# A convolution kernel's parameter ladder and first table put under an order searched offline

## The chip, the cores and the metric

The program runs on one core of one Trainium2 chip. The metric is device time in microseconds (us). Four runs of the kernel before spread from 529.19 to 531.01, so differences of a few microseconds in 530 need several runs.

Five engines matter here. PE multiplies matrices (PEld is its loading of weights), DVE works on vectors, ACT works elementwise and evacuates PE's results, POOL and SP do little (before, POOL is busy 2% of the span and the page lists no busy time for SP). In these traces an engine takes the instructions of its queue in their order, and the queues meet at semaphores: before, DVE waits 2.08 us at its first statistics, up to 9.29 us, and the square of sh behind them, whose input was ready at 7.87, starts at 11.08. So the order in a queue decides what waits for what.

## The reference

The program is a stack of four layers on a sequence of 2048 rows and 512 channels: a long convolution, a local attention, and both again. Each layer works on the normalized rows and adds its result to them.

```
x = x + conv(layernorm(x))       # this change: layernorm and the start of this layer
x = x + attention(layernorm(x))
x = x + conv(layernorm(x))
x = x + attention(layernorm(x))

# the convolution's kernel, for each channel d and lag l, over 128 modes n:
K[d, l] = Re( sum over n of  C[d,n] * dt[d]*B[d,n] * exp(dt[d]*(A_re + i*A_im)[d,n] * l) )
# and the convolution itself by Fourier transforms of length 2L
```

## The kernel before

The first 64 us prepare two things. The **ladder** squares the complex base exp(dt A) ten times (`lad`, 128 x 512 numbers each for the real and imaginary part) and casts each power into multipliers (`MU`, `MUA`, `MUB`, `MP`, `MH`). The **tables** hold powers by lag for 64 channels at a time, eight tables in all; a table is a seed, four doubling levels (two products and a sum each), a fifth "high" level, and three products `y`. PE then contracts a table with 256 small matmuls (`psk`) to 64 rows of the convolution's kernel. A table lies in one of two buffers:

```python
class Tables:
    def __init__(self, nc, tc, es, M, cb):
        self.tt = es.enter_context(tc.tile_pool(name="t_t", bufs=2))   # two buffers for eight tables
    ...
    def seed(self, hc):                    # the first DVE operation on table hc
        self.nc.vector.tensor_copy(self.T[hc][:, 1, :, :, 0, :]..., self.cb[:, hc]...)
```

The work from the tables to the end of the convolution is written as a plan: operations with an engine, a duration, and the buffers they take and drop. An offline search picked an order and, for some, one of two engines; the kernel only carries the numbers of the operations in that order.

```python
def tables(hc):
    o = pl.op("G", 0.4, lambda: T.ones(hc), take=[("T", hc)])          # takes one of the two buffers
    o = [o, pl.op("V", 0.15, lambda: T.seed(hc), o)]
    for lev in range(4):
        ab = pl.op("V", ..., lambda lev=lev: T.level(hc, lev), o)
        ...                                                            # levels 2 to 4: sum on DVE, or on PE and ACT
def contract(hc):
    for half in range(2):
        a = pl.op("P", 2.9, mm, ...)                                    # 128 matmuls
        e = moved(pl, nc, ("psk", hc, half), 0.5, 0.61, evac, a, ...,
                  drop=[("psk", hc, half)] + ([("T", hc)] if half else []))   # the buffer is free here
```

Ladder and norms were outside the plan, in hand-written order; tables 0 and 1 were both in it, level by level in turn.

Of the kernel before, what the change touches and what calls it, by code (L numbers as in the profile page):

```python
# [192 lines left out]
def load_params(nc, pp, prm):  # L193
# [16 lines left out]
    "33 58 34 59 35 60 36 61 37 62 38 63 39 64 40 66 43 1 44 55 4 49 56 50 5 67 57 2 7 8 10 68 83 32 11 12 69 22 18 "  # L210
    "84 86 80 19 74 20 87 81 90 89 78 21 155 15 79 76 16 27 25 91 77 92 26 93 82 94 115 95 96 97 118 116 100 101 30 "
    "119 189 121 123 112 31 156 126 124 190 132 106 127 129 154 130 191 108 133 113 109 145 139 110 146 135 111 147 "
    "192 136 150 114 151 137 148 193 214 138 194 195 196 152 215 199 157 153 163 217 158 200 164 211 159 218 205 161 "
    "160 259 220 142 324 162 260 143 209 212 175 171 210 166 180 172 207 167 173 261 208 168 262 263 174 178 213 169 "
    "186 183 179 185 292 264 284 184 187 221 293 188 265 237 298 285 295 299 301 266 287 296 323 269 302 308 270 223 "
    "288 318 358 281 239 225 290 359 229 313 227 360 231 241 325 275 243 311 233 235 361 321 245 312 303 277 322 362 "
    "279 278 282 316 280 247 317 363 326 251 283 332 249 333 253 327 364 383 254 365 368 256 384 369 328 257 330 386 "
    "380 329 331 374 334 350 387 306 381 351 432 389 497 340 307 352 341 353 342 433 375 345 357 343 337 434 346 355 "
    "382 465 338 347 466 468 354 435 457 414 469 348 436 390 356 471 458 437 460 472 438 439 442 392 461 531 463 498 "
    "416 532 443 396 394 533 474 454 418 475 496 534 406 420 477 481 492 478 535 408 486 493 398 536 479 410 448 412 "  # L220
    "494 480 400 495 537 484 449 404 402 489 485 456 425 490 499 426 538 503 455 500 422 504 505 423 501 502 541 559 "
    "506 517 429 562 507 560 542 556 553 513 547 563 520 514 565 608 523 521 510 554 524 529 515 511 525 548 516 527 "
    "526 555 528 609 611 610 530 613 566 612 615 614 629 616 558 622 567 557 617 569 630 635 574 570 572 632 636 582 "
    "575 583 577 431 633 620 580 590 578 585 621 430 625 586 627 588 638 626 661 628 591 648 639 662 593 428 649 641 "
    "594 669 651 596 642 670 598 652 654 599 601 655 605 644 604 602 664 645 606 657 607 665 647 667 672 677 658 675 "
    "685 660 679 673 686 681 688 683 692 689 699 696 700 693 697 702 694 703",
    "39 20 40 1 21 22 41 2 58 3 23 59 42 4 30 10 60 11 61 6 7 16 66 28 13 17 64 35 26 49 14 24 194 68 32 43 101 62 "
    "195 45 47 126 72 102 79 127 54 76 80 104 51 77 85 105 75 82 86 107 83 228 110 108 229 112 113 244 88 115 248 245 "
    "89 119 246 249 230 120 247 94 232 122 252 231 233 250 91 96 253 236 92 251 97 141 234 256 237 142 235 98 258 254 "
    "259 257 100 255 116 240 242 123 117 238 243 125 241 239 169 260 223 170 264 262 224 272 263 265 138 274 284 273 "  # L230
    "139 157 285 275 278 158 129 132 286 130 268 279 133 135 287 266 269 136 151 288 267 270 152 160 289 154 276 161 "
    "271 290 156 277 291 163 280 296 144 164 332 172 282 145 283 334 176 147 333 319 338 177 148 335 320 149 166 340 "
    "339 167 188 321 344 341 189 191 322 336 345 192 185 323 201 337 346 186 197 324 173 342 198 347 174 325 297 343 "
    "179 348 326 298 180 365 350 182 371 351 366 183 367 202 352 200 372 353 203 368 331 220 354 379 217 221 211 355 "
    "375 218 380 212 208 356 369 357 376 205 209 303 370 206 358 214 226 311 304 215 359 227 312 309 364 310 301 299 "
    "302 305 300 307 306 385 308 391 316 313 389 318 386 373 315 392 377 390 395 378 374 381 393 396 383 397 394 384 "
    "399 398 429 387 400 430 388 421 401 431 407 404 403 432 409 408 406 433 422 411 434 410 413 412 499 437 415 414 "
    "500 438 417 416 439 497 419 418 440 498 420 441 442 503 423 456 446 501 426 425 444 504 443 502 428 457 448 445 "
    "505 447 450 507 449 452 508 451 454 525 506 461 509 465 453 510 526 455 511 463 462 512 475 458 466 464 469 476 "
    "473 470 513 467 460 474 471 521 519 481 479 517 468 480 522 485 482 472 515 486 483 523 477 489 491 487 484 524 "  # L240
    "527 493 557 528 529 553 530 558 531 573 494 545 554 532 575 533 488 572 586 534 546 587 574 535 492 561 576 588 "
    "490 549 577 536 495 563 578 540 537 607 589 542 590 580 609 550 598 543 562 599 582 604 591 600 564 605 608 565 "
    "618 606 610 619 611 612 620 621 613 566 622 614 617 623 567 624 570 628 568 625",
    "5 9 14 6 4 15 11 7 3 1 12 8 2 0 13 10 17 21 25 105 22 19 26 29 33 30 109 34 111 106 45 113 117 39 114 121 119 37 "
    "123 38 193 42 197 195 48 124 199 201 49 205 133 203 206 81 51 59 82 214 84 70 60 130 281 71 52 136 127 85 282 53 "
    "73 137 208 86 56 57 285 74 88 211 169 90 62 286 158 217 170 139 75 159 147 63 79 140 220 77 172 148 141 221 64 "
    "173 143 146 174 66 69 289 223 178 101 176 293 290 103 92 150 294 95 98 93 224 96 242 151 99 225 161 243 302 152 "
    "227 245 229 296 253 156 162 154 231 299 254 246 163 232 256 305 247 165 234 167 330 249 251 183 257 331 308 235 "
    "184 333 258 309 319 260 334 262 341 311 320 186 342 312 180 187 189 181 236 190 313 322 240 238 335 315 323 317 "
    "276 339 344 324 337 277 264 326 279 268 328 265 347 269 267 272 350 348 271 273 361 355 362 352 275 356 358 353 "  # L250
    "359",
    "1 20 2 3 58 21 4 22 59 39 8 6 11 9 40 13 23 60 41 24 16 26 14 30 32 61 42 28 17 197 47 49 45 35 79 62 198 64 43 "
    "126 68 80 51 66 76 127 54 101 77 104 102 75 85 105 72 82 86 107 83 228 88 108 229 90 91 230 110 93 232 231 94 "
    "112 233 244 113 96 245 236 97 114 119 234 237 248 120 235 98 246 122 252 249 99 247 250 144 242 251 253 238 243 "
    "116 146 254 239 123 118 256 255 166 125 258 257 167 169 240 259 171 241 160 260 182 161 264 262 183 266 263 265 "
    "157 272 284 267 158 129 285 273 278 130 163 151 286 164 274 172 279 152 148 287 270 275 149 132 288 271 268 133 "
    "138 289 154 276 139 269 147 155 290 277 291 135 280 185 296 136 332 173 186 282 338 174 333 283 194 346 339 319 "
    "195 176 340 347 177 179 320 344 341 180 191 200 321 342 345 192 205 336 343 206 188 334 337 189 211 201 297 335 "
    "212 214 348 322 323 298 215 305 324 350 223 303 351 306 224 299 352 325 304 353 326 300 354 331 202 355 309 217 "
    "203 307 310 218 141 356 311 357 308 142 301 208 358 365 209 302 226 359 312 369 366 313 220 364 316 370 315 375 "  # L260
    "221 318 385 376 391 386 227 387 392 393 388 389 394 377 390 399 378 395 400 397 396 407 398 379 404 401 367 406 "
    "380 408 373 403 368 371 374 419 372 381 415 520 383 417 416 384 521 420 429 413 511 430 499 411 414 431 512 418 "
    "432 500 505 433 421 434 412 506 409 435 422 436 410 441 528 448 423 442 501 426 425 450 454 443 502 449 529 428 "
    "455 446 451 444 516 513 456 447 452 445 461 457 467 453 517 462 458 468 469 524 473 463 460 475 474 525 470 464 "
    "476 465 560 471 530 479 466 472 481 480 485 477 482 483 486 489 548 493 484 491 549 487 492 550 539 531 540 488 "
    "532 543 535 544 494 536 490 554 495 547 555 561 556 566 562 567 568 572",
]


def flat(xs):  # L270
    return [z for x in xs for z in (flat(x) if isinstance(x, (list, tuple, set)) else [x])]


class Plan:


# [42 lines left out]
class Multipliers:  # L319
# [8 lines left out]
    def slots(self, k):  # L328
# [7 lines left out]
        if k % 6 == 0:  # L336
            return [self.one[:, :, 1 - k // 6].unsqueeze(3), self.base[1][:, 0, :, 1 - k // 6]]
        return [self.base[0][:, k % 6 - 1, :, 1 - k // 6], self.base[1][:, k % 6, :, 1 - k // 6]]


def ladder(nc, pp, pst, identf, raw, M, cb, fill):

# [72 lines left out]
    for i in range(11):  # L415
# [7 lines left out]
        if i == 0:  # L423
            coefs()
# [1167 lines left out]
```

## Time and profile before

| Before | us |
|---|---|
| time, median of 4 runs beside the changed kernel | 530.39 (529.19 to 531.01) |
| span of the profiled run | 528.9 |
| table 0 complete on DVE | 63.9 |
| first PE transposes of the attention layer | 226.1 |

The prediction below shows the busy times and the timelines of DVE and ACT. Three more views are needed. First the busy time by stretch (length, then busy PE, PEld, DVE, ACT, POOL with counts, then granted clock, DMA share, GB/s):

```profile
226.00:530.00 304.00, 268.64 (x1880) 142.71 (x1893) 263.50 (x451) 166.65 (x264) 4.78 (x40) 0.97 0.33 74
```

This is the stretch from the attention layer on, which the change should leave alone. Second, the waits of DVE, with the total, the number and the longest:

```profile
DVE prod L1241 <- ACT kT L1195: 15.0, 2, 7.6
...
DVE ln_st_b L150 <- ACT X L856: 3.3, 3, 1.9
```

Third, PE's timeline (start, length, operation, idle before and what ended it):

```profile
63.67 1.99 PE L711 MATMUL ps_s<-X,sb_F 128*128 128x128 bf16 x16 [6.31 <-ACT Z L716]
65.59 0.24 PE L558 MATMUL psk<-Ttab 128*32 128x64 bf16 x4
...
69.11 0.22 PE L558 MATMUL psk<-Ttab 128*32 128x64 bf16 x4 [0.74 <-issue]
```

The contraction of table 0 starts at 65.59, and DVE has table 1 to work on meanwhile. Inside the contraction PE stands still once, for 0.74 us, with nothing visible to wait for ("issue").

### The profile page before, as it was taken

To read this page: it belongs to the slowest core of one execution; us is meant where nothing else is said; L and a number is where in the kernel's file an instruction comes from. 1 tells how busy PE (TensorE), PEld (TensorE's weight loads), DVE (VectorE), ACT (ScalarE), POOL (GpSimd) and SP (SyncE) were. 2 spreads that over 40 slices of the span, in tenths; PEclk is the share of its full clock that TensorE was granted. 3 is DMA by queue.
4 is the path that set the end of the run, shared out by engine and by line. 5 is a ranking of instruction groups with operands and counts; after the bars stand their busy time and mean duration, and the time that the engine had idled before them with its cause. 6 is when DMAs were issued, how large, how long until landed. Compare 5 with 4: busy or idle time off the path is not lost.

```text
span 528.9 us, 11855 instructions
## 1 busy us (share of the span) xinstructions
PE 404.1 (76%) x4929; PEld 238.6 (45%) x4943; DVE 475.5 (90%) x803; ACT 339.2 (64%) x505; POOL 12.9 (2%) x62
## 2 busy tenths in 40 slices
PE   0201367799878779689999788969995999996896
PEld 0100235466655547443456234555673333652352
DVE  4999999999999998749899998889989497999995
ACT  3999965887857668662766137989995336651230
POOL 0000000000000004000000000000000000000000
PEclk9999997979989999979999999999996999999999
DMA  8300083249135343460011522779501400223242
GB/s 264 153 1 0 0 141 90 61 114 163 43 114 110 62 142 106 139 120 31 0 61 50 91 49 40 197 204 159 81 2 35 85 30 32 71 48 61 40 130 90
DMA packets 88922, 45.08 MB, mean 85 GB/s; under 512 B 74923, under 2 KB 81068, under 8 KB 88612
## 3 DMA queue, kind: packets, MB, share of 16 engines
q1 hardware_dynamic: 87284, 43.93, 34.8%
q8 instruction: 38, 0.62, 0.5%
q10 hardware_dynamic: 1584, 0.39, 0.4%
q14 instruction: 16, 0.13, 0.1%
HBM read 15.77 MB, written 8.13 MB: 45 GB/s over the span
## 4 chain that ended last, share of the span: by engine, by line
PE 34%; DVE 33%; ACT 10%; issue 9%; DMA 3%; SPq 0%; POOL 0%; DVEq 0%; ACTq 0%
PE ps_qk L1190 11%; DVE prod L1353 7%; PE ps_v L1210 4%; PE Lp L1251 3%; DVE Y2tab L545 3%; DVE Ttab L545 3%; DVE ln_st_b L150 2%; DVE Ttab L488 2%; DVE Ttab L481 2%; DMA Kt<-kt_scratch 2%; DVE Ttab L480 2%; PE ps_o L1426 2%; DVE prod L1241 2%; ACT X L598 1%; PE po L1374 1%
## 5 line engine op out<-in xcount | busy, mean ns | idle before, releaser
L1241 DVE TENSOR_TENSOR prod<-qT,kT 128x2048 bf16<-128x2048 bf16 (+1 forms) x80 | 77.1, 1005 | 15.7 <-ACT kT L1195 15.0
L1353 DVE TENSOR_TENSOR prod<-VX,L 128x2048 bf16<-128x2048 bf16 (+2 forms) x96 | 77.4, 861 | 1.7 <-PE po L1374 0.9
L1190 PE MATMUL ps_qk<-xnT,wqk 128*128 128x512 bf16 x256 | 63.7, 388 | 0.1
L1369 PE MATMUL po<-prod,sb_ident 128*128 128x512 bf16 x216 | 54.5, 378 | 8.1 <-DVE prod L1353 4.9
L1369 PEld LDWEIGHTS <-sb_ident 128*128 128x128 bf16 x224 | 21.4, 97 | 35.6 <-issue 11.7
L1190 PEld LDWEIGHTS <-wqk 128*128 128x128 bf16 x256 | 22.8, 100 | 32.1 <-issue 11.6
L1210 PE MATMUL ps_v<-wv,xnT 128*128 128x256 bf16 x256 | 34.6, 282 | 0.8 <-ACT xnT L1168 0.6
L1389 ACT CAST ot<-po 128x1024 bf16<-128x1024 f32 x14 | 13.6, 1014 | 29.7 <-PE po L1369 29.7
L520 PE MATMUL ps_sum<-Ttab,sb_ident 128*128 128x512 bf16 x18 | 8.3, 459 | 31.0 <-DVE Ttab L480 27.7
L1251 PE MATMUL Lp<-prod,sb_bones 128*32 128x512 bf16 x256 | 28.6, 388 | 4.3 <-DVE prod L1241 4.2
L1215 ACT CAST VX<-ps_v 128x512 bf16<-128x512 f32 x32 | 18.8, 587 | 17.2 <-PE ps_v L1210 17.2
L716 ACT CAST Z<-ps_s 128x1024 bf16<-128x1024 f32 (+1 forms) x32 | 29.4, 995 | 0.5 <-PE ps_s L711 0.4
L561 PE MATMUL psk<-Y2tab,Ttab 128*32 128x48 bf16 x1024 | 21.5, 198 | 9.5 <-issue 8.5
L545 DVE TENSOR_TENSOR Ttab<-Ttab,MPA 128x2048 bf16<-128x2048 bf16 (+2 forms) x20 | 28.4, 1434 | 0.3
L558 PE MATMUL psk<-Ttab 128*32 128x64 bf16 x1024 | 21.5, 203 | 9.3 <-DVE Ttab L545 6.1
L1210 PEld LDWEIGHTS <-xnT 128*128 128x128 bf16 x256 | 24.0, 100 | 9.8 <-issue 4.6
L1426 PE MATMUL ps_o<-wo_t,oT 128*128 128x512 bf16 x108 | 27.5, 379 | 0.3 <-issue 0.2
L545 DVE TENSOR_TENSOR Y2tab<-Ttab,MPB 128x6144 bf16<-128x6144 bf16 (+1 forms) x13 | 27.2, 2120 | 0.0
L1195 ACT CAST qT<-ps_qk 128x512 bf16<-128x512 f32 x24 | 14.0, 584 | 19.4 <-PE ps_qk L1190 19.4
L150 DVE BATCH_NORM_STATS2 ln_st_b<-X 128x6 f32<-128x128 bf16 (+2 forms) x80 | 22.9, 355 | 3.7 <-ACT X L856 3.3
L1195 ACT CAST kT<-ps_qk 128x512 bf16<-128x512 f32 x26 | 15.2, 584 | 16.5 <-PE ps_qk L1190 16.5
L558 PEld LDWEIGHTS <-Ttab 128*32 128x32 bf16 x1024 | 19.4, 102 | 13.1 <-issue 12.2
(218 smaller groups left out, 1022.4 us busy)
## 6 DMA issues: line engine op xcount, KB each, us to landing
X<-in_A_u_dram SPq DMA_DIRECT2D x8, 512.0 KB, 5.1
kt_scratch<-sp_k SPq DMA_DIRECT2D x16, 256.0 KB, 2.7
Kt<-kt_scratch SPq DMA_DIRECT2D x16, 256.0 KB, 6.0
out_dram<-X SPq DMA_DIRECT2D x4, 512.0 KB, 2.7
k_scratch<-KTq SPq DMA_DIRECT2D x7, 256.0 KB, 2.7
KT<-k_scratch SPq DMA_DIRECT2D x7, 256.0 KB, 2.9
VX<-VX SPq DMA_DIRECT2D x4, 448.0 KB, 3.8
kT<-kT SPq DMA_DIRECT2D x8, 192.0 KB, 2.3
```

Source lines behind the costliest of these rows:

```text
L150: self.nc.vector.bn_stats(self.st[:, j, part, :], X[:, j, a:b])
L545: nc.vector.tensor_tensor(d, src.to_broadcast([128, c, n, 2 * EYB]), mm.to_broadcast([128, c * n, EYB, 2]), ALU.mult)
L558: nc.tensor.matmul(o.rearrange("e (s i) -> e s i", s=2), xs, T[:, 1:3, h, m // 2, :, t], start=(m == 0), stop=False, skip_group_check=True)
L716: nc.scalar.copy(box["Z", kind, dc][:, 0:n // 8, :, jq * 32:(jq + 1) * 32].rearrange("p g r k -> p r g k"), box.pop(("s1", kind, dc, jq))[ ...
L1190: nc.tensor.matmul(ps[:], wqk[:, ct, f0:f0 + 128], xnT[:, 4 * s:4 * s + 4, ct, :], start=(ct == 0), stop=(ct == 3))
L1195: copy((qT, kT)[which][fp][:, f2, o:o + 512], box.pop(("qk", which, fp, f2, s))[:])
L1210: nc.tensor.matmul(ps[:, jj].rearrange("p t h d -> p (t h d)"), xnT[:, j + jj, ct, :], wv[:, ct, fp * 256:(fp + 1) * 256], start=(ct == 0) ...
L1241: nc.vector.tensor_tensor(pr[:, 0:n2], qT[fp][:, a:a + n2, j0 * 128:j0 * 128 + 1024], kT[fp][:, a:a + n2, c0:c0 + 1024], ALU.mult)
L1251: nc.tensor.matmul(Lp[r0:r0 + 32, w // 4, :], bones[:, w % 4, :], pr[:, f2 - a, hb * 512:(hb + 1) * 512], start=(n == 1), stop=(n == 4), s ...
L1353: nc.vector.tensor_tensor(p2[:, 0:nj].rearrange("p j t d h -> p (j t) d h"), VX[:, fp, NV + a:NV + a + nj].rearrange("p j (t d h) -> p (j ...
L1369: nc.tensor.matmul(po[:, c:c + 512], ident[:], p2[:, k + j:k + j + 2].rearrange("p j t d h -> p (j t d h)"), start=(n == 1), stop=(n == W))
L1426: nc.tensor.matmul(ps, box["oT"][:, ft // 2, j, ft % 2, :], wo_t[:, ft, :], start=(ft == 0 and not res), stop=(ft == 3))
```

## The change

The intent is to give the search the start of the program as well: the ladder, the first LayerNorm and table 0 become a plan of their own (`prepare`), with the casts of the multipliers free to run on ACT or DVE, and norms too. Table 0 is built in two halves, to start before all multipliers are there. All later orders were searched again.

```diff
-def ladder(nc, pp, pst, identf, raw, M, cb, fill):
-    ... 100 lines in fixed order ...
+def prepare(nc, pp, pst, raw, identf, M, cb, T, ln, X):
+    pl = Plan(ptq=2, sq=2, lad=3)
+    ...
+        if ma.shape[3] == 2:
+            A = pl.either(("ma", i), lambda: [act(a_copy(0)), act(a_copy(1))], lambda: follow(act(a_copy(0)), twin()),
+                          lambda: follow(ve(v_copy(0)), twin()))
+    ...
+    for lev in range(4):
+        for x in (1, 0):                                   # table 0 in two halves
+            a = vec(2 * us, lambda lev=lev, x=x: T.level(0, lev, x, x + 1), o[x], casts[...])
+            o[x] = vec(us, lambda lev=lev, x=x: T.level_sum(0, lev, x, x + 1), a)
 ORDERS = [
-    "33 58 34 59 35 60 36 61 37 62 38 63 ..."              # tables 0 and 1 in turn, then the convolution
+    "297 1 2 3 5 7 8 24 9 20 10 21 25 ..."                 # new: the preparation
+    "35 67 3 6 36 68 4 37 60 69 7 38 70 39 71 63 ..."      # tables 1 and 2 in turn, then the convolution
     ... three more orders, all new ...
```

In the second list 35 to 59 build table 1, 60 to 65 contract table 0, and 67 to 91 build table 2.

## The prediction

> **What bounds the kernel now.** I read the page's busy times and the 40 slices first, then busy time by stretch, then the timelines of DVE, ACT and PE over the first 100 us, and last the chain of waits there, because the change rebuilds that part.
>
> ```profile
> PE 404.1 (76%) x4929; PEld 238.6 (45%) x4943; DVE 475.5 (90%) x803; ACT 339.2 (64%) x505; POOL 12.9 (2%) x62
> DVE  4999999999999998749899998889989497999995
> ACT  3999965887857668662766137989995336651230
> ```
>
> DVE is at 90% of the span. A slice is 13.2 us, and DVE is at 9 from the second slice to the sixteenth, which is the parameter ladder, the tables and the first convolution. ACT is full only in slices two to five.
>
> ```profile
> 13.00:26.00 13.00, 3.82 (x15) 2.28 (x13) 13.00 (x23) 12.05 (x20) 0.00 (x0) 1.00 0.40 164
> 40.00:64.00 24.00, 5.25 (x24) 2.54 (x25) 23.62 (x31) 23.97 (x39) 0.00 (x0) 1.00 0.00 0
> 64.00:106.00 42.00, 29.80 (x929) 19.95 (x927) 40.75 (x43) 29.24 (x35) 0.71 (x6) 0.90 0.45 93
> 146.00:186.00 40.00, 30.46 (x741) 23.20 (x739) 39.83 (x52) 27.08 (x35) 0.24 (x2) 0.92 0.40 94
> ```
>
> The columns after the length are busy PE, weight loads, DVE, ACT and POOL with counts, then clock, DMA share and GB/s. In the ladder (13 to 64 us) DVE and ACT are both full; from 64 to about 215 us DVE alone is full. So here the time is DVE's work plus DVE's idle time, and only these two count. The idle is small and sits at the start:
>
> ```profile
> 4.43 0.17 DVE L346 CAST dtf<-dtb 128x4 f32<-128x4 bf16 x1 [4.43 <-ACT dtb L344]
> 6.51 0.69 DVE L361 TENSOR_TENSOR ws<-tb,rnd 128x512 f32<-128x512 f32 x1
> 9.29 1.88 DVE L150 BATCH_NORM_STATS2 ln_st_a<-X 128x6 f32<-128x512 bf16 x3 [2.08 <-DMA X<-in_A_u_dram]
> 11.08 0.67 DVE L367 TENSOR_TENSOR cs<-sh 128x512 f32<-128x512 f32 x1
> ...
> 61.58 2.29 DVE L545 TENSOR_TENSOR Ttab<-Ttab,MPA 128x4096 bf16<-128x4096 bf16 x1
> 64.63 1.23 DVE L480 TENSOR_TENSOR Ttab<-Ttab,MUA 128x2048 bf16<-128x2048 bf16 x1 [0.77 <-ACT Ttab L525]
> ```
>
> The last operation of table 0 starts at 61.58 and frees DVE at about 63.8. Inside the ladder DVE has by then also done much of table 1 (below). It then waits 0.77 us for ACT, which is late because of its own queue:
>
> ```profile
> 13.57 0.58 ACT L378 COPY LAM<-ptq 128x512 f32<-128x512 f32 x1 [5.18 <-PE ptq L377]
> 51.21 11.37 ACT L598 ACTIVATE X<-X,ln_nb_a,ln_rstd_a 128x512 bf16<-128x512 bf16 x16
> 62.61 1.01 ACT L716 CAST Z<-ps_s 128x1024 bf16<-128x1024 f32 x1
> ```
>
> [...] the statistics that wait until 9.29 us hold back the square of sh, though sh was finished at 7.9 (ACT's timeline: start 7.24, 0.63 long). [...] the trace has 0.67 to 0.69. [...] In a full queue the starts are closer than the durations: 0.60 us for these, 1.14 for bf16 of 2048 (1.22 long), 0.60 for 1024, 0.34 for 512, 0.30 for 256 at level 0. I count with these paces. [...] PE's gaps called "issue" inside the table contractions (0.74 us at 68.4, 2.44 us at 80.0) are not hidden; the trace does not say whether fetching causes them.
>
> **The change part by part**, from the order in which the built instructions stand.
>
> 1. *Start.* Three of the four products of C and B move ahead of the statistics, into the idle 2.08 us, and a fourth just ahead of the last subtraction for Sin. That one waits for B_im (issued at 1.88, landing 5.0 us later, so about 6.9), so Sin starts about 8.2 instead of 7.24. Counting on: subtraction 7.5 to 8.2, three products to about 9.3, one statistic, then the square of sh at about 9.9 and the second quadrant product finished near 13.3 instead of 13.9. Gain: about 2.1 us of DVE idle filled, and ACT's first evacuation 0.6 us earlier.
> 2. *Table 0 in halves.* Levels 0 to 3 have 24 operations in place of 12. Level 0: 6 x 0.20 (estimate for 128 elements, between the 0.11 of the seed copy and 0.30) against 0.92; level 1: 6 x 0.20 (estimate) against 3 x 0.34; level 2: 6 x 0.34 against 3 x 0.60; level 3: 6 x 0.60 against 3 x 1.14. That is 8.0 against 7.2: 0.9 us more.
> 3. *Alternatives taken.* The search used little of its freedom: one of the multipliers' casts (MUA) becomes a DVE copy of the first half (0.3), and two of 16 norms go to DVE (2 x 0.3). DVE +0.9 us; ACT loses 0.5 + 2 x 0.71 = 1.9 us. ACT's norms then end near 60 instead of 62.6, so the wait of 0.77 us goes.
> 4. *Tables 1 to 7.* On DVE the level-3 sums go from 7 to 5 and the level-2 sums from 6 to 5; PE and ACT do them instead (20 more ps_sum matmuls, 6 more half evacuations). DVE loses 2 x 1.2 + 0.6 = 3.0 us.
> 5. *The new order has a fault.* Right behind the last product of table 0 stands the seed of table 2, then tables 1 and 2 level by level, interleaved. But there are two table buffers, and table 2 lives in table 0's. Its seed carries a wait on PE: all 256 matmuls of table 0's contraction must have read the buffer, and they cannot start before that same last product. The search seems to have missed it: the marker that takes buffer 0 for the new plan (operation 0) stands at place 360 of 476 in the list, so in the search's books both buffers were free. DVE's queue being strict, all of table 1 waits too. Before, DVE had table 1 to work on through the contraction. Cost, from before's PE timeline: first half 65.59 to 67.17 (1.58), second half 67.96 to 70.20, less a gap of 0.74 (1.50). Back to back 3.1, plus the start and the release (about 0.1 each) and one gap: about 4.0 us of empty DVE.
> 6. *The other plans* (end of the convolution, both attention layers, second convolution) have newly searched orders with nearly the same operations: two q evacuations from DVE to ACT, three Z evacuations the other way, one softmax sum off PE. I read no sum from these; I set -0.5 us, with a spread of 2.
>
> Sum by DVE time. Before, at 63.8 table 0 was done, and 3.25 us of table 1: seed 0.11, level 0 0.92, level 1 1.02, two level-2 products 1.2. So table 0 alone costs up to about 60.6. After: 60.6 - 2.1 + 0.9 + 0.9 = 60.3, plus about 0.8 for statistics and aggregations of single rows now alternating instead of 16 aggregations in one run (0.066 apart), and half-table sums that wait for the product right ahead: about 61.2. Empty until 65.2. Before at 65.2 had 3.25 + 0.6 us more done; after has 3.0 us less left. Behind by 0.8 us at about 215 us. With part 6: 530.25 + 0.8 - 0.5 = about 530.5. I take 0.5 off that, since an order searched as a whole may also shorten the end of the convolution, where DVE waits 3.3 us for ACT's X and 1.0 for PE's vp: **530.0 us**.
>
> **Rivals.**
> - *The stall is hidden.* If contraction 0 started early, or the seed did not wait on it, DVE would lose nothing, and the whole -4 us would show: about 526. For it: the search was made for a gain. Against it: the wait on PE in the built program, and a contraction that needs table 0's last product.
> - *A longer stall.* If a gap such as the 2.44 us at 80.03 falls into contraction 0, it adds directly to DVE's idle: about 532. The chain shows that such gaps sit on the path already:
>
> ```profile
> 76.46 2.21 DVE Ttab L545
> 78.67 0.04 issue
> 78.71 0.22 PE psk L558 x4
> ...
> 80.03 2.44 issue
> ```
>
> - *ACT becomes the bound.* More sums go through PE and ACT, and level 3 of table 2 waits for ACT's evacuation of level 2. From 64 to 106 us ACT is busy 29 of 42 us, and between level 2's product and its use there stand 2.9 us of DVE work against about 2.2 for PE (0.9) and two evacuations (about 1.1). Should each of four such waits miss by half a microsecond: +2, about 532.
> - *The other plans gain more than I give them.* ACT's 15.0 us of DVE waiting for kT in the first attention layer is slack that a better order could use: -3, about 527. Nothing in the diff aims at it.
>
> **Range and chances.** Part 5 is uncertain by +2.4 and -0.8, part 6 by 2, the rest by 1: 526.5 to 533.5. A change of 2% is 10.6 us. Even without the stall the listed gains make 4 to 5, and two large gaps make about +5. Faster 0.04, same 0.92, slower 0.04.
>
> **What would show it.** In the profile after: DVE's idle before the first statistics near 0 instead of 2.08; the square of sh near 9.9; the first statistics' wait gone; table 0's last product ending near 61; right behind it a DVE gap of 3.3 to 5.7 us whose releaser is PE's psk, before the seed of table 2; ACT's 14 norms ending near 60; no wait of DVE for ACT's ps_sum evacuation longer than 0.5 us; DVE otherwise full up to about 215. Wrong if that gap is missing or below 2 us, if the ladder itself has DVE waits above 1 us for ACT or PE, or if the span from 226 us on differs by more than 3 us from before's 303.

"0.67 to 0.69" and the 0.60 "for these" are DVE's fp32 products of 512 elements per partition. What a table cut in halves pays is priced in part 2 from the paces: half the elements take more than half the time (0.34 us for 512 against 0.60 for 1024). That DVE's queue is strict (part 5) rests on the wait until 9.29 us. In both traces each of the six `ACT_TABLE_LOAD` takes 1.28 us, three of them in the first 50 us (before, one starts at 5.93 and the next operation at 7.24).

## The result, and the profile after

| | before | after |
|---|---|---|
| time, median | 530.39 (4 runs) | 532.91 (4 runs, 532.27 to 533.82) |
| profiled span | 528.9 | 531.2 |
| granted clock | 0.963 | 0.961 |
| table 0 complete on DVE | 63.9 | 60.3 |
| first transposes of the attention layer | 226.1 | 228.8 |

The ratio of after to before is 1.0051, with a 95% interval of 1.0028 to 1.0075. By the 2% rule it is "same"; the interval says slower by half a percent.

The page of the kernel after, its busy times and DVE's 40 slices of 13.3 us:

```profile
PE 408.5 (77%) x4955; PEld 240.0 (45%) x4955; DVE 476.7 (90%) x820; ACT 340.4 (64%) x506; POOL 13.0 (2%) x62
...
DVE  5999599999999998758899998899989498999995
```

DVE has 1.2 us more work and 17 more instructions in all. The new thing is the 5 in the fifth slice (53 to 66 us). DVE's timeline shows the two things that the change did to it, at the start and behind table 0:

```profile
6.96 0.69 DVE L488 TENSOR_TENSOR t<-raw_C_re,raw_B_im 128x512 f32<-128x512 bf16 x1 [0.45 <-DMA raw_B_im<-in_A_B_im_dram]
...
9.98 0.69 DVE L150 BATCH_NORM_STATS2 ln_st_a<-X 128x6 f32<-128x512 bf16 x1
10.58 0.68 DVE L488 TENSOR_TENSOR sh<-sh 128x512 f32<-128x512 f32 x1
...
58.03 2.29 DVE L452 TENSOR_TENSOR Ttab<-Ttab,MPA 128x4096 bf16<-128x4096 bf16 x1
66.21 0.23 DVE L363 COPY Ttab<-cb 128x128 bf16<-128x128 bf16 x1 [5.89 <-PE psk L468]
```

The first statistics no longer wait. Table 0's last product ends at 58.03 + 2.29 = 60.32, 3.5 us earlier than before. Then DVE is empty for 5.89 us: the next instruction in its queue is the seed of table 2, which needs table 0's buffer, and PE is still reading that. PE and ACT at the same time:

```profile
59.99 1.22 PE L790 MATMUL ps_s<-X,sb_F 128*128 128x128 bf16 x10 [2.73 <-ACT X L636]
61.14 0.24 PE L465 MATMUL psk<-Ttab 128*32 128x64 bf16 x4
...
65.42 0.20 PE L468 MATMUL psk<-Y2tab,Ttab 128*32 128x48 bf16 x3 [2.09 <-issue]
```

```profile
50.66 9.98 ACT L636 ACTIVATE X<-X,ln_nb_a,ln_rstd_a 128x512 bf16<-128x512 bf16 x14
```

The stall has parts that can be read off. PE could have begun at 60.32, but until 59.99 its queue stood at a spectrum matmul that waited for a row which ACT normed next to last; the ten matmuls left took to 61.14: 0.82 us. The matmuls before the gap take to 63.3 (2.2 us), the gap 2.1, the rest 0.7, the release 0.1.

By stretch, then DVE's waits:

```profile
64.00:106.00 42.00, 29.30 (x729) 18.52 (x730) 39.34 (x48) 24.84 (x30) 0.82 (x6) 0.80 0.42 90
...
226.00:530.00 304.00, 271.02 (x1893) 143.69 (x1893) 270.03 (x481) 167.36 (x266) 4.78 (x40) 0.97 0.32 73
```

```profile
DVE Ttab L363 <- PE psk L468: 5.9, 1, 5.9
...
DVE ln_st_b L150 <- ACT X L935: 4.4, 3, 2.2
```

From the first transposes of the attention layer to the end it is 528.9 - 226.1 = 302.8 us before and 531.2 - 228.8 = 302.4 after. So the whole loss lies ahead of 229 us. PE's granted clock from 64 to 106 us is lower than before (0.80 against 0.90). After the stall, though, DVE has no wait above 0.25 us until 167.9, so in that stretch nothing is lost by it.

**A ledger of DVE up to those transposes.** I counted every DVE operation in both traces up to there, each until its end or until the next one starts, by tile and size; what is left is idle. (The names in the rows are the prediction's parts.)

| Term | predicted | measured |
|---|---|---|
| idle up to the end of table 0, without the first 4.4 us | -2.1 | 3.04 to 1.48: -1.6 |
| table 0 in halves, casts and norms, single aggregations | 0.9 + 0.9 + 0.8 = +2.6 | 0.2 + 0.9 + 0.3 = +1.4 |
| sums of tables 1 to 7 moved off DVE | -3.0 | -3.2 |
| wait before level 3 of table 1 | -0.8 | -0.8 |
| stall before the seed of table 2 | +4.0 | +5.9 |
| other waits up to the end of the convolution | -0.5 | +1.9 idle, -0.9 mostly for operations that now come later: +1.0 |
| everything from the attention layer on | -0.5 | -0.4 |
| sum | -0.3 | +2.3 |

The sum of the measured terms is the difference of the profiled spans, 531.2 - 528.9 = 2.3.

### The profile page after: what moved, and what is told of

The parts are those of the page before. It is cut to its first block, busy times and chain, and to the rows that moved or that the text cites. A ratio compares the mean times of both kernels' runs of the same rounds, so it can differ in the third digit from the quotient of the medians.

```text
span 531.2 us, 11916 instructions
## 1 busy us (share of the span) xinstructions
PE 408.5 (77%) x4955; PEld 240.0 (45%) x4955; DVE 476.7 (90%) x820; ACT 340.4 (64%) x506; POOL 13.0 (2%) x62
## 5 line engine op out<-in xcount | busy, mean ns | idle before, releaser
L1449 PE MATMUL po<-prod,sb_ident 128*128 128x512 bf16 x224 | 55.9, 388 | 8.1 <-DVE prod L1433 6.2
L790 PE MATMUL ps_s<-X,sb_F 128*128 128x128 bf16 x128 | 10.7, 246 | 30.3 <-ACT X L636 28.1
L790 PEld LDWEIGHTS <-sb_F 128*128 128x128 bf16 x256 | 16.0, 104 | 36.5 <-issue 33.2
L1275 ACT CAST qT<-ps_qk 128x512 bf16<-128x512 f32 x26 | 15.2, 584 | 15.9 <-PE ps_qk L1270 15.9
L531 PE MATMUL ptq<-identf,quad 128*128 128x128 f32 x16 | 4.4, 430 | 26.7 <-ACT MPA L552 13.5
```

Source lines behind the costliest of these rows:

```text
L790: nc.tensor.matmul(o, F1[:, j, r, :], rhs(j), start=True, stop=not dk)
L1275: copy((qT, kT)[which][fp][:, f2, o:o + 512], box.pop(("qk", which, fp, f2, s))[:])
L1449: nc.tensor.matmul(po[:, c:c + 512], ident[:], p2[:, k + j:k + j + 2].rearrange("p j t d h -> p (j t d h)"), start=(n == 1), stop=(n == W))
```

## The experiments

Nine runs, eight kernels, all correct, in three batches, each batch beside the kernel before on the same chip (medians of before: 530.4 in the first batch, 530.0 in the second, 530.3 in the third). The theory: the change is a gain of a few microseconds that the stall before the seed of table 2 eats. The rivals: new orders elsewhere lose the time, or the preparation is worse than it looks.

A third table buffer was meant to take the wait away directly, but its build stops: it reports that the preparation's pool asks for 57.28 KB per partition and that 37.6 KB are left.

### e1: table 1 ahead of the seed of table 2

```diff
-"35 67 3 6 36 68 4 37 60 69 7 38 70 39 71 63 40 61 72 41 73 9 64 42 12 10 66 75 45 ..."
+"35 67 3 6 36 4 37 60 7 38 39 63 40 61 41 9 64 42 12 10 66 45 47 49 68 69 70 48 71 72 50 73 75 57 51 ..."
```

The operations are the same; those of table 1 up to the level-3 products (36 to 42 and 45, with PE's matmuls 47 and 49 for the level-3 sum) now stand ahead of the seed of table 2 (68).

> The changed kernel with table 1 built up to its level-3 products before table 2 is begun; every operation and engine the same. Theory A (the seed of table 2 waits for table 0's contraction, and the 5.89 us are paid in full because DVE bounds this part): the wait of DVE for psk before the seed of table 2 falls from 5.89 us to below 1 us, and the time falls by 5 to 6 us, to about 527.5. Rival B (the end of the convolution is bound by a chain through PE and ACT, so that the stall is paid back there): the wait goes too, but the time stays within 1.5 us of 532.9.

Measured: 529.14 us (527.16 to 530.36), ratio to before 0.9964 (0.9931 to 0.9998), first transposes at 225.0. DVE's timeline of e1:

```profile
60.94 0.42 DVE L329 TENSOR_TENSOR Ttab<-Ttab,MUA 128x512 bf16<-128x512 bf16 x1
...
66.54 0.22 DVE L305 COPY Ttab<-cb 128x128 bf16<-128x128 bf16 x1
...
115.61 1.23 DVE L329 TENSOR_TENSOR Ttab<-Ttab,MUA 128x2048 bf16<-128x2048 bf16 x1 [1.30 <-ACT Ttab L374]
```

The last product of table 0 ends at 61.0 and DVE runs straight into table 1 (its seed and level 0 had already run inside the ladder, from 38.1 on: the built queue does not keep the two lists apart, and in the changed kernel the seed alone stands there; so table 0 ends 0.7 us later here), and at 66.54 the seed of table 2 finds its buffer free. PE's contraction is not faster than in the changed kernel, with a gap of 1.35 us where that had 2.09; nobody waits for it any more. Of 5.9 us, 3.7 arrive at the transposes (228.8 to 225.0). The rest comes back as the 1.30 us at 115.6, and as small waits and operations that now stand ahead of the transposes (0.9 together). The wait went as both theories said. The time fell by 3.8 us: less than theory A's 5 to 6, far more than rival B allows.

### e2: two levels of table 1 ahead of the seed

```diff
-"35 67 3 6 36 68 4 37 60 69 7 38 70 39 71 63 40 61 72 41 ..."
+"35 67 3 6 36 4 37 60 7 38 39 63 40 68 69 70 71 61 72 41 ..."
```

> A dose: only levels 0 and 1 of table 1 (1.9 us of DVE work) stand before the seed of table 2. Theory A: the wait falls from 5.89 to about 4.0 us and the time by about 1.9 us, to about 531.0. Rival B: the wait falls the same, the time does not.

Measured: 532.41 us (532.39 to 532.53), ratio 1.003 (1.0006 to 1.0054). The seed of table 2 in e2:

```profile
66.62 0.23 DVE L305 COPY Ttab<-cb 128x128 bf16<-128x128 bf16 x1 [4.26 <-PE psk L410]
```

The wait shrinks from 5.89 to 4.26 us, but the time by only 0.5 us, 1.4 short of the 1.9 that theory A expected. Here too level 0 of table 1 ran inside the ladder: table 0 ended at 61.18 instead of 60.32, so the seed starts 0.4 us later than in the changed kernel (66.62 against 66.21). And DVE's idle up to the transposes falls by 0.7 us, not 1.6, so part of a removed wait returns later, as in e1. As a dose the run agrees with theory A in the wait, not in the time.

### e3: the old order of the convolution behind the new preparation

```diff
-ORDERS[1] = "35 67 3 6 36 68 4 37 60 69 ..."
+ORDERS[1] = "0 " + the order before, renumbered, without the operations of table 0
```

> New preparation and table 0, but tables 1 to 7 and the convolution in the order and on the engines of the kernel before (operations numbered over, table 0's taken out). Theory A: no wait for psk before the seed of table 2, and 3.0 us more DVE work than in the changed kernel: 532.9 - 5.9 + 3.0 = about 530.0. Rival B: about 532.5. Rival C (the preparation itself is slower than before, in ways the sum of DVE work misses): 532 or more even without the wait.

Measured: 535.50 us (535.20 to 535.95), ratio 1.0089. A clear miss. Three timelines of e3, of DVE, ACT and PE:

```profile
68.74 1.23 DVE L329 TENSOR_TENSOR Ttab<-Ttab,MUA 128x2048 bf16<-128x2048 bf16 x1 [5.30 <-ACT Ttab L374]
```

```profile
66.72 1.01 ACT L737 CAST Z<-ps_s 128x1024 bf16<-128x1024 f32 x1 [5.85 <-issue]
```

```profile
62.99 0.59 PE L369 MATMUL ps_sum<-Ttab,sb_ident 128*128 128x512 bf16 x1 [31.89 <-DVE Ttab L329]
...
64.73 1.91 PE L732 MATMUL ps_s<-X,sb_F 128*128 128x128 bf16 x16
```

The old order was made for a ladder in which table 1's lower levels were already built by 49 us. Here they come after table 0, at 61 to 63. PE's queue holds table 1's sum first, so the spectrum matmuls behind it start at 64.73 instead of 52; ACT's queue holds the evacuation of that spectrum (66.72) ahead of table 1's (67.63); and DVE waits 5.30 us at the end of this chain. One stall took the place of the other. (ACT's idle is put down to "issue"; what it waited for is PE's `ps_s`, which ends at 64.73 + 1.91 = 66.64, 0.08 us before ACT's start.) The ledger adds that the old order keeps three more sums on DVE, 3.0 us of work (2.45 at 2048 elements, 0.58 at 1024), which confirms part 4 of the prediction from the other side. So e3 does not isolate the preparation, as it was meant to.

### e4: the kernel before with the three later orders alone

```diff
-ORDERS = [before[0], before[1], before[2], before[3]]
+ORDERS = [before[0], after[2], after[3], after[4]]
```

> The kernel before with nothing changed but the three later orders (both attention layers, second convolution), taken from the changed kernel. The two traces have the same length from the first transposes of the attention layer to the end (302.8 and 302.4 us), so theory A expects no change: 530.4 within 0.7. My prediction had -0.5 for them. Rival D (the later orders lose what the new preparation wins): 532 or more.

Measured: 531.00 us (530.86 to 531.49), ratio 1.0005 (0.998 to 1.0029). No gain or loss shows; the interval leaves room for 1 us of gain or 1.5 us of loss. This agrees with 302.8 against 302.4 us in the two profiles.

### e5: 360 idle PE instructions in the ladder

```diff
                 nc.tensor.transpose(pt[:, t, :], quad[:, t, q, :], identf[:])
+            if q == 3:
+                pad = pst.tile([128, 8], F32, name="pad", tag="pad", bufs=1)
+                for _ in range(180):
+                    nc.tensor.matmul(pad[:], small[:], small[:, 0:8], start=True, stop=True)
```

This asks what the gap inside the contraction is. I numbered PE's instructions in each trace in order of time. In the first 110 us the gaps inside contractions that are put down to "issue" sit at the numbers 449, 961 before and 449, 1217, 1729 after (within one or two): 449 plus a multiple of 256. And in the stretch from 61 to 66 us of the kernel after, the DMA view has one single packet:

```profile
DMA packets 1, 0.02 MB, mean 3 GB/s; under 512 B 0, under 2 KB 0, under 8 KB 0
...
q8 instruction: 1, 0.02, 1.6%
```

> The changed kernel with 360 extra PE instructions (180 small matmuls with their weight loads, into a spare PSUM tile) while PE is idle in the ladder. Nothing of the result changes. Theory F: the empty 2.1 us inside contraction 0 come from fetching PE's program, because in both kernels the gaps sit at the instruction numbers 449 + 256k of PE's program. Then here the gap moves with the count: 360 = 256 + 104, so it sits 104 instructions earlier inside the contraction (after about 278 of its 512 instructions instead of about 382), at number 705. The gap's length stays 1.5 to 2.3 us, DVE's stall before the seed of table 2 stays 5.3 to 6.3 us, the time stays within 1 us of the changed kernel's 532.9. Rival G: the gap belongs to a place of the contraction (a wait on its own data or on an evacuation); then it stays after about 382 instructions of the contraction.

Measured (one look): 532.59 us. PE's timeline of e5:

```profile
63.88 0.24 PE L465 MATMUL psk<-Ttab 128*32 128x64 bf16 x3 [0.76 <-issue]
```

The gap moved to number 705, exactly as counted, 278 instructions into the contraction instead of 382. So it belongs to the count of PE's program and not to a place in the contraction. Most multiples of 256 show no such gap: PE's gaps over 0.5 us that are put down to "issue" are 7 in the whole kernel before, with 0.7 to 2.4 us of idle PE each, against 38 packets of 16 KB that its queue "instruction" moves. Here the gap was shorter (0.76 us) and DVE's stall 5.04 us, under the expected 5.3 to 6.3; inside contraction 0 it was 2.09 us in the changed kernel, 1.35 in e1, 1.28 in e3 and 1.36 in e6, so the length varies. The DMA records say more. The packet shown above is of queue "instruction", 16 KB long, and starts at 62.77; PE runs dry at 63.33 and goes on at 65.42, 2.65 us after the packet's start. After each of the 7 such gaps before and the 8 after, PE goes on 2.4 to 2.8 us after the start of such a packet. So in these two traces a gap is the longer the later its packet starts: packets 0.2 to 0.3 us before PE runs dry stand with gaps of 2.2 to 2.4 us, packets 1.4 to 2.0 us before it with 0.7 to 1.1. That PE waits for the packet was not shown by an experiment; why a packet starts when it does was not examined, nor why most multiples of 256 show no gap.

### e6: ACT's norms in the order in which PE needs the rows

```diff
-"... 269 284 ... 291 289 279 267 276 ... 295 277 265 285 287 273 293 271 281"
+"... 265 284 ... 267 269 271 273 276 ... 277 279 281 285 287 289 291 293 295"
```

> The changed kernel with ACT's 14 norms sorted by row group, so that the rows that PE's first two spectra need (0 to 7) come first; DVE's two norms stay where they are. In the changed kernel PE's queue stood at a spectrum matmul until 59.99 us for a norm that ACT did next to last, and contraction 0 behind it started at 61.14, 0.8 us after table 0 was finished at 60.32. Theory: with the norms sorted the contraction starts within 0.2 us of table 0's end, DVE's stall falls from 5.9 to about 5.1 us, and the time from 532.9 to about 532.1. Rival: the contraction's start was set by something else; stall and time stay as they were (5.9 us, 532.9).

Measured: 532.28 us (531.48 to 532.85), ratio 1.0046 (1.0022 to 1.0071), stall 4.83 us:

```profile
60.33 0.25 PE L407 MATMUL psk<-Ttab 128*32 128x64 bf16 x4 [4.24 <-DVE Ttab L394]
```

The contraction now begins when table 0's last product is done, 0.8 us earlier, and its releaser is DVE. This confirms the late start as a part of the stall. The gap was shorter too (1.36 us), but the matmuls on either side of it took 0.4 us longer (60.33 to 62.7 and 64.1 to 65.0), so that the stall is 1.06 us shorter in all. The time is near the expected 532.1, but a gain over the changed kernel is not shown: their ratios to before are 1.0046 and 1.0051, with intervals that overlap almost wholly.

### e7: two more moves in the order of e1

```diff
 # PE's sum of table 4's level 2 (244) and its evacuation (245) one place earlier
-"... 160 242 146 155 190 161 244 162 156 150 165 245 198 ..."
+"... 160 242 146 244 155 190 161 162 245 156 150 165 198 ..."
 # the end: second half of the last channels (625 to 635) ahead of evacuations
-"... 567 562 598 406 602 563 604 565 615 638 603 605 568 625 639 616 570 626 ..."
+"... 567 625 562 598 626 406 602 563 604 565 615 628 638 603 605 568 639 616 629 ..."
```

> The order of e1 (table 1 ahead of the seed of table 2; 529.1 us) with two more moves: the PE sum of table 4's level 2 and its evacuation one place earlier (there DVE waited 1.30 us at 115.6), and at the end of the convolution the second half of the last 32 channels (its rows, first and second transform) moved ahead of evacuations that nobody waits for yet (there DVE waited 2.25 us for ACT's X at 209.3 and 0.4 twice). Theory H: these waits were queue order alone, so the first goes (-1.1) and the end shortens by about 2.5: 525.5, first transposes of the attention layer near 221.5 instead of 225.0. Rival J: ACT, busy 93% from 198 to 214, is the bound there; only the first wait goes and the end gains under 0.5: about 527.8.

Measured: 529.25 us (528.85 to 531.86), ratio 0.9996 (0.9966 to 1.0026). The wait at 115.6 is gone, but neither theory has the end right. DVE's timeline of e7 (the profiled run is the slowest of the four):

```profile
81.83 3.42 DVE L394 TENSOR_TENSOR Ttab<-Ttab,MPA 128x4096 bf16<-128x4096 bf16 x2 [1.85 <-PE ps_sum L370]
...
212.26 0.69 DVE L823 TENSOR_TENSOR pa<-sp_u,sp_k 128x1024 bf16<-128x1024 bf16 x1 [3.84 <-PE vp L847]
```

There are two product buffers (`pa`), and my order asked for a third product before PE had read the first. The 1.85 us at 81.8 is a different matter, below.

### e8 and e9: the order of e1 with more rounds, and with the first move of e7 alone

e8 is the kernel of e1, unchanged; e9 is e1 with only the first of the two edits shown under e7.

> The order of e1 once more, unchanged, with more rounds and beside e9 on the same chip. In e1 it stood at 529.1 us with a ratio of 0.9964 and an interval that just missed 1. Theory: with DVE's stall gone, the rest of the change is worth its terms as measured: the ledger of the changed kernel (+2.3 us over before) less the 3.7 us that e1 took off at the first transposes, so about -1.4 us: ratio 0.9973, between 0.995 and 0.999. Rival: e1's gain was drift between chips; then the ratio is 1.000 or above.

> The order of e1 with one of the two moves of e7: PE's sum of table 4's level 2 and ACT's evacuation one place earlier. In e7 the wait of 1.30 us at 115.6 was gone, while the other move, at the end of the convolution, made DVE wait 3.8 us for a product buffer. Theory: without that second move the gain of the first stays: DVE has no wait above 0.5 us between 60 and 190 us, and the time is 0.8 to 1.2 us below e8: about 528.0. Rival: the 1.3 us reappear in a later wait (PE or ACT reach the end no earlier), and e9 equals e8 within 0.4 us.

Measured: e8 529.15 us (528.22 to 530.24, 6 runs), ratio 0.9981 (0.9969 to 0.9993). e9 528.76 us (526.76 to 531.79, 6 runs), ratio 0.9977 (0.9953 to 1.0001). So the order of e1 beats the kernel before by 0.2%, as e8's theory said, and the interval of e8 excludes 1. By the medians of different batches it beats the changed kernel by some 3.8 us. Whether e9 is better than e8 is not settled: its runs spread over 5 us, its median is 0.4 us lower, and its profile has a wait that its theory excluded. Its profile, the slowest of the six (e8's is the fastest of its six), shows one reason; by stretch, then PE's timeline of the sums there:

```profile
76.00:80.00 4.00, 3.26 (x9) 1.13 (x8) 4.00 (x2) 1.93 (x2) 0.00 (x0) 0.58 0.62 117
```

```profile
77.72 0.63 PE L370 MATMUL ps_sum<-Ttab,sb_ident 128*128 128x512 bf16 x1
78.15 0.63 PE L369 MATMUL ps_sum<-Ttab,sb_ident 128*128 128x512 bf16 x1
...
80.40 0.38 PE L369 MATMUL ps_sum<-Ttab,sb_ident 128*128 128x512 bf16 x1
80.62 0.38 PE L370 MATMUL ps_sum<-Ttab,sb_ident 128*128 128x512 bf16 x1
```

The granted clock is 0.58 from 76 to 80 us, and the sums start 0.43 us apart there (77.30 to 79.86), against 0.22 once the clock is back (0.99 from 80 to 84 us). DVE then waits 1.77 us for the last of them at 81.90. e1 and e8 have the same instructions up to there; their clock in these 4 us was 1.00 and the wait 0.22. e7's sums too start 0.43 us apart (77.15 to 79.71), so the dip shows in two of these four profiles. In the order of e1 DVE thus waits 0.22 us for PE's sums of table 1's high level even at a clock of 1.00, and with the dip 1.77 (e9) or 1.85 (e7), 1.6 us more. How often the dip comes, and how much of e9's spread it makes, was not measured.

## Why the prediction was right or wrong

The range (526.5 to 533.5) held, and so did "within 2%": 532.9. The point was 2.9 us too low, and against the medians even the sign was wrong (530.39 to 532.91, where it said -0.3). That the range held owes something to luck: by the ledger the parts ahead of the stall came out 0.9 us better than said, the stall 1.9 and the end of the convolution 1.5 us worse; without those 0.9 the time would have been near 533.8, above the range. And "within 2%", 10.6 us, was an easy call: it would have held with no stall as well.

- **Part 1, the start.** The mechanism held: no wait at the first statistics, square of sh at 10.6 (said 9.9). It gave 1.6 of 2.1 us, because the first product itself waits 0.45 us for B_im, whose landing the prediction had worked out but not charged to DVE.
- **Parts 2 and 3.** The halves cost 0.2 instead of 0.9 us in the count of the two traces; the estimate of 0.20 us for small operations held (starts 0.17 apart at 128 elements, 0.20 at 256), so the excess lies mostly in pricing the old, larger operations at their best pace (before, the level-3 sum of table 0 started 1.26 us ahead of the next operation, not 1.14). The single aggregations cost 0.3, not 0.8. So table 0 ended at 60.3, not 61.2. The norms ended at 50.66 + 9.98 = 60.6, and no evacuation made DVE wait at level 3 of table 1, as said.
- **Part 4.** Said -3.0; measured -3.2, and +3.0 when e3 took it back.
- **Part 5, the stall.** It is there, before the seed of table 2, released by PE's `psk`, as said. The term "about 4.0 us of empty DVE" was mis-sized: it measured 5.9. The working assumed a contraction that starts 0.1 us after table 0, and one gap of 0.74. The start was 0.8 late because of the order of ACT's norms (e6 takes that away), and the gap was 2.1. That a longer gap would add directly was the rival "A longer stall", which said 532 and was nearest. e1 shows that the stall was a matter of order: with the same operations it is gone.
- **Part 6 and the last 0.5.** The later plans are neutral, as set (-0.4; e4 shows it alone). The credit for a shorter end of the convolution was wrong in sign: other waits grew by 1.9 us (0.72 at 168.6 and 0.42 at 208.7 for `pa`, and 1.1 more for ACT's X), of which 0.9 is offset by operations that come later.
- **The rivals.** "The stall is hidden" fell with the 5.89 us. "ACT becomes the bound" fell too: ACT is busy 24.84 of 42 us in the stretch after, less than before, and no level-3 wait is longer than 0.5 us. "The other plans gain more" fell with e4.

What stays open: why the last expected 1 to 2 us do not arrive in e1 and e2 can be listed (new waits of 1.3 and less) but was not removed by experiment, since e7 and e9 ran into other waits. That the wrong order came from an error in the search's book-keeping of buffer 0 was only argued.

## What to carry to other kernels

When a plan is reordered, look at the head of each queue for the first instruction that takes a shared buffer: here everything behind it waited for the buffer's last reader, 5.89 us, even work on table 1 that could run (e1 runs it there, from 60.94 to 66.54). Before trusting such a wait's size, add what stands in the reader's own queue ahead of it (0.82 us here), and its gaps (2.09). And an order made for one start of a program (e3, a wait of 5.30 us in place of 5.89) or one that asks for more buffers than there are (e7, 3.84 us for a third product in two buffers) can lose as much as it was meant to gain.
